# Pooling sums of K and V on GpSimd, written chunk by chunk instead of level by level

## The chip, the cores and the metric

One NeuronCore of a Trainium2 chip runs the whole program in one launch. The metric is the device time of that launch in microseconds; lower is better. PE is TensorE, DVE is VectorE, ACT is ScalarE, POOL is GpSimd and SP is the engine whose queue issues most of the transfers.

## The reference

Three steps, all in float32: an attention whose keys and values are first pooled, a mixture of experts with one expert for each token, and a second feed-forward with a maximum of three products. Only the first step matters for the change. Eight batches, eight heads, 576 rows of 64 values; every eight neighbouring rows of K and of V are averaged into one, which leaves 72 rows for each head.

```python
def _attn_ref(q, k, v):
    B, H, S, D = q.shape            # 8, 8, 576, 64
    pool = 8
    Sp = S // pool                  # 72
    k_p = k.reshape(B, H, Sp, pool, D).mean(axis=3)
    v_p = v.reshape(B, H, Sp, pool, D).mean(axis=3)
    scores = 1.0 / np.sqrt(D) * np.matmul(q, k_p.transpose(0, 1, 3, 2))
    ...
    return np.matmul(attn, v_p)
```

## The kernel before

The program has three stages: attention with the routing of tokens to experts (the first 200 us or so), the expert products, and the second feed-forward. Nothing is scheduled by a tool: each engine runs its instructions in the order in which the code writes them, and waits on semaphores where one needs another's result.

**Attention.** The 4608 tokens are 36 tiles of 128 rows, and the loop at L1477 runs as a pipeline over them. In one turn it writes the scores of one tile (`stage_s`, L415, tile `psc` on PE, then the maximum `mx` and the difference `sh` on DVE), the transposes of an older one (`stage_a`, `paT`), those of a new one (`stage_q`, `pqT`), and the product with V of the oldest (`stage_x`, L482, `pav` on PE, then `rs`, `x`, `dt`, `lg` on DVE). PE may write the next `psc` only when DVE has made `sh` out of the old one, and the next `pav` only when DVE has made `dt`.

**Pooling.** The 576 pooled rows of one batch, 72 for each of 8 heads, lie as four chunks of 128 partitions and a fifth of 64. `load_rows` (L188) brings the raw rows into `kraw` and `vraw`, shape [128, 5, 8, 64]: chunk, the eight rows to be added, 64 values. They are added by halving: the upper four rows onto the lower four (`w` is 4), then two onto two, then one onto one, whose result goes to `kp` (or `vp`). V of all batches and K of batches 2 to 7 are pooled on POOL: `pool_k2` (L263) and `pool_v` (L275). K of batches 0 and 1 is pooled on DVE. `spread_v` (L284) multiplies the pooled V into `vbd`, five POOL instructions for each batch. PE then transposes `kp` into `ptk` (L313, for batches 2 and up) and multiplies with `vbd` in `pav` (L490). The loop calls these steps of a batch at turns that the table at L1464 to L1469 sets: for batch b its pooling stands five turns ahead of the first tile that needs it.

**Routing.** Among the DVE instructions of a turn the loop pushes single steps of the routing (`fill`, L910): constants first, then for each group of tiles (tiles 0 to 8, 9 to 17, 18 to 23) the steps of `rank_steps` (L600). They work on small tiles in SBUF: `lg` scaled and reduced by its maximum, `wt`, `wm`, `oh`, a copy of `oh` into `pre`, four prefix additions `pre<-pre`, later `rk`, `rank`, `ri`, `lb`, `slot`. When the slots of a group are ready, POOL makes one `ohs` for each tile of the group (L656). After the third group an early part of the routing reads the `ohs` of 24 tiles (L751) and starts the loads of the experts' weights.

**The queue of SP.** It is in order too: K and V of a later batch, q, and the stores of finished tiles. A load of `vraw` waits until POOL has read the buffer's old content.

Of the kernel before, what the change touches and what calls it, by code (L numbers as in the profile page):

```python
# [14 lines left out]
A = mybir.AluOpType  # L15
# [6 lines left out]
def attention_moe_moe_kernel(  # L22
# [24 lines left out]
    nc = tc.nc  # L47
    dbg = dbg or {}

    P = 128  # L50
# [65 lines left out]
    if True:  # L116
# [61 lines left out]
        if True:  # L178

            RC = [P, P, P, P, 64]  # L180
# [67 lines left out]
            def prep_steps(b):  # L248
                kt, vt = kv[b]
                kb, vb = kbds[b % 3], vbds[b % 3]  # L250
                kp = qp.tile([P, 5, 2, D], F32, tag="kp", name=f"kp{b}")
                vp = kp[:, :, 1, :] if b > 1 else qp.tile([P, 5, D], F32, tag="vp", name=f"vp{b}")
# [8 lines left out]
                        pool_k(c)  # L261

                def pool_k2():  # L263
                    for c0, c1, n in ((0, 4, P), (4, 5, RC[4])):
                        for w in (4, 2, 1):
                            dst = kt[0:n, c0:c1, 0:w, :] if w > 1 else kp[0:n, c0:c1, 0:1, :]
                            nc.gpsimd.tensor_tensor(
                                dst, kt[0:n, c0:c1, 0:w, :], kt[0:n, c0:c1, w : 2 * w, :], op=A.add
                            )

                def dup_k():
                    for c0, c1, n in ((0, 3, P), (3, 4, KC[3]), (4, 5, KC[4])):
                        nc.scalar.copy(kp[0:n, c0:c1, 1, :], kp[0:n, c0:c1, 0, :])

                def pool_v(c0, c1, n):  # L275
                    for w in (4, 2, 1):
                        for a0 in range(c0, c1, 2) if w == 4 else (c0,):
                            a1 = min(a0 + 2, c1) if w == 4 else c1
                            dst = vt[0:n, a0:a1, 0:w, :] if w > 1 else vp[0:n, a0:a1, :].unsqueeze(2)
                            nc.gpsimd.tensor_tensor(  # L280
                                dst, vt[0:n, a0:a1, 0:w, :], vt[0:n, a0:a1, w : 2 * w, :], op=A.add
                            )

                def spread_v():  # L284
                    for c, (h0, h1) in enumerate(HS):
# [74 lines left out]
                if b == 0:  # L360
                    return [
                        lambda: (pool_all(), dup_k(), trans_k(range(4), 0, 7), trans_k([4], 7, 8)),
                        lambda: (pool_v(0, 4, P), pool_v(4, 5, 64), spread_v()),
                        lambda: (trans_v(0, 4), trans_v(4, 5)),
                        lambda: vdot(),
                    ]
                if b == 1:
                    pk = [lambda c=c: pool_k(c) for c in range(5)]
                    pk += [lambda: (pool_v(0, 4, P), pool_v(4, 5, 64))]
                else:  # L370
                    return [
                        lambda: (pool_k2(), pool_v(0, 4, P), pool_v(4, 5, 64)),
                        spread_v,
                        lambda: trans_kv(range(4), 0),
                        lambda: trans_kv([4], 4 * P),
                        vdot,
                    ]
# [1425 lines left out]
```

## Time and profile before

| | |
|---|---|
| median of 3 runs | 1264.73 us (1262.85 to 1265.89) |
| the profiled execution's own time | 1260.98 us |
| its span | 1259.2 us |
| PE busy | 1215.6 us, 97% of the span |
| DVE busy | 799.2 us, 63% |
| ACT busy | 580.5 us, 46% |
| POOL busy | 318.9 us, 25%, 383 instructions |
| mean granted clock of TensorE | 0.991 |

The profile is one execution of the program. Its page gives the busy time of each engine and its share of the span; other views order the same instructions by time, by group or by stretch, and name for each idle time of an engine the instruction that ended it. The profiled execution was shorter than each of the three timed runs. Shares over the whole span hide the stages: POOL's 25% are over 85% in each stretch of 15 to 17 us between 30 and 92 us, and little after 180 us.

### The profile page before, as it was taken

To read this page: it belongs to the slowest core of one execution; us is meant where nothing else is said; L and a number is where in the kernel's file an instruction comes from. 1 tells how busy PE (TensorE), PEld (TensorE's weight loads), DVE (VectorE), ACT (ScalarE), POOL (GpSimd) and SP (SyncE) were. 2 spreads that over 40 slices of the span, in tenths; PEclk is the share of its full clock that TensorE was granted. 3 is DMA by queue.
4 is the path that set the end of the run, shared out by engine and by line. 5 is a ranking of instruction groups with operands and counts; after the bars stand their busy time and mean duration, and the time that the engine had idled before them with its cause. 6 is when DMAs were issued, how large, how long until landed. Compare 5 with 4: busy or idle time off the path is not lost. (4 is left out here: it accounts for less than half of the span.)

```text
span 1259.2 us, 22318 instructions
## 1 busy us (share of the span) xinstructions
PE 1215.6 (97%) x8251; PEld 1158.0 (92%) x8251; DVE 799.2 (63%) x1575; ACT 580.5 (46%) x1040; POOL 318.9 (25%) x383
## 2 busy tenths in 40 slices
PE   5899899999999999999999999999999999999995
PEld 4788789999999999999999998998998998998994
DVE  6676886797889999898764446345445454454450
ACT  3466465545666676666655333323223323223221
POOL 6985553420212212222000302103103004004001
PEclk9899999999999999999999999999999999999998
DMA  9968246423976445844619666475564673773721
GB/s 252 267 202 236 97 138 217 151 85 32 298 262 226 164 143 203 283 151 137 207 51 350 241 238 242 160 262 205 207 239 182 220 264 153 258 263 124 253 108 52
DMA packets 98038, 246.21 MB, mean 196 GB/s; under 512 B 17100, under 2 KB 58106, under 8 KB 89858
## 3 DMA queue, kind: packets, MB, share of 16 engines
q1 hardware_dynamic: 84770, 189.09, 44.5%
q0 software_dynamic: 13152, 55.62, 13.3%
q8 instruction: 67, 1.10, 0.4%
q14 instruction: 49, 0.40, 0.1%
HBM read 252.23 MB, written 46.98 MB: 238 GB/s over the span
## 5 line engine op out<-in xcount | busy, mean ns | idle before, releaser
L1617 PE MATMUL p<-yhi,wt 128*128 128x384 f32 x1512 | 387.2, 336 | 0.0
L1617 PEld LDWEIGHTS p<-yhi,wt 128*128 128x128 f32 x1512 | 273.4, 188 | 0.6
L1617 PE MATMUL p<-ylo,wt 128*128 128x384 f32 x756 | 254.0, 336 | 0.0
L1625 ACT COPY s<-p 128x384 f32<-128x384 f32 x162 | 77.8, 480 | 221.1 <-PE p L1617 216.8
L1104 PE MATMUL py<-hhi,whi 128*128 128x256 f32 x576 | 164.6, 286 | 0.0
L1104 PE MATMUL py<-hhi,wlo 128*128 128x256 f32 x576 | 163.1, 283 | 1.6 <-DVE wlo L1036 1.6
L1056 PE MATMUL ph<-xhi,whi 128*128 128x256 f32 x576 | 163.8, 284 | 0.7 <-DVE hlo L1072 0.7
L1056 PE MATMUL ph<-xhi,wlo 128*128 128x256 f32 x576 | 163.0, 283 | 0.7 <-DVE wlo L1036 0.7
L1056 PE MATMUL ph<-xlo,whi 128*128 128x256 f32 x576 | 163.0, 283 | 0.0
L1104 PE MATMUL py<-hlo,whi 128*128 128x256 f32 x576 | 162.9, 283 | 0.0
L1617 PEld LDWEIGHTS p<-ylo,wt 128*128 128x128 f32 x756 | 142.1, 188 | 0.5
L1646 DVE TENSOR_TENSOR blk<-p,s 128x384 f32<-128x384 f32 x108 | 59.7, 553 | 113.9 <-PE p L1617 113.9
L1602 POOL DMA_INDIRECT gt<-gbuf,ix x26 | 37.0, 1424 | 312.1 <-DMA ix<-idbuf 305.7
L1104 PEld LDWEIGHTS py<-hhi,wlo 128*128 128x128 f32 x576 | 110.4, 192 | 1.8 <-DVE wlo L1036 1.8
L1056 PEld LDWEIGHTS ph<-xhi,whi 128*128 128x128 f32 x576 | 110.5, 192 | 1.2 <-DVE hlo L1072 0.9
L1056 PEld LDWEIGHTS ph<-xhi,wlo 128*128 128x128 f32 x576 | 110.5, 192 | 0.9 <-DVE wlo L1036 0.9
L1056 PEld LDWEIGHTS ph<-xlo,whi 128*128 128x128 f32 x576 | 110.5, 192 | 0.0
L1104 PEld LDWEIGHTS py<-hlo,whi 128*128 128x128 f32 x576 | 110.5, 192 | 0.0
L1104 PEld LDWEIGHTS py<-hhi,whi 128*128 128x128 f32 x576 | 110.4, 192 | 0.0
L1036 DVE TENSOR_TENSOR wlo<-w2raw,whi 128x1024 fp32r<-128x1024 f32 x84 | 102.2, 1221 | 8.8 <-ACT whi L1034 8.7
L1036 DVE TENSOR_TENSOR wlo<-w1raw,whi 128x1024 fp32r<-128x1024 f32 x67 | 81.8, 1220 | 27.6 <-ACT whi L1034 26.5
L1034 ACT CAST whi<-w2raw 128x1024 fp32r<-128x1024 f32 x88 | 91.8, 1044 | 7.7 <-PE py L1104 4.7
(316 smaller groups left out, 2280.8 us busy)
## 6 DMA issues: line engine op xcount, KB each, us to landing
wt<-wdram SPq DMA_DIRECT2D x51, 1792.0 KB
w1raw<-in_moe_w_dram SPq DMA_DIRECT2D x88, 512.0 KB
w2raw<-in_moe_w_dram SPq DMA_DIRECT2D x88, 512.0 KB
wdram<-wst POOLq DMA_DIRECT2D x9, 1792.0 KB
ybuf<-yo SPq DMA_DIRECT2D x40, 256.0 KB
cvraw<-in_moe_w_dram POOLq DMA_DIRECT2D x36, 256.0 KB
vraw<-in_v_dram SPq DMA_DIRECT2D x8, 1024.0 KB
xbuf<-x SPq DMA_DIRECT2D x16, 512.0 KB
```

The lines of the kernel that those rows point to most:

```text
L1034: nc.scalar.copy(hi, src)
L1036: eng.tensor_tensor(lo, src, hi.bitcast(F32), op=A.subtract)
L1056: nc.tensor.matmul(ps[:, f, :], a_[:, c, fs], b_[:, c, :], start=(n == 0), stop=(n == 3 * DC - 1))
L1104: nc.tensor.matmul(py[:, c // 2, (c % 2) * 256 : (c % 2 + 1) * 256], a_[:, f, c * P : (c + 1) * P], b_[:, f, :], start=(piece == 0 and f = ...
L1602: nc.gpsimd.indirect_dma_start(out=gt[g][:, j : j + 1], out_offset=None, in_=gbuf[:, :], in_offset=bass.IndirectOffsetOnAxis(ap=cols[j], a ...
L1617: nc.tensor.matmul(ps, a_, b_, start=(start and c + n == 0), stop=(c == 1 and n == 2), skip_group_check=True)
L1625: nc.scalar.copy(t, ps)
L1646: tt(src, add[0], add[1], op=A.add)
```

## The change

`pool_k2` and `pool_v` keep the same additions on the same engine. Before, one instruction did a level of the halving for all four full chunks (the first level of V for two chunks at a time). Now each chunk goes through its three levels before the next one begins. The two functions have five lines less, so that later lines have numbers smaller by 5 in the changed kernel.

```diff
--- before.py
+++ after.py
@@ -261,25 +261,20 @@
                         pool_k(c)
 
                 def pool_k2():
-                    for c0, c1, n in ((0, 4, P), (4, 5, RC[4])):
+                    for c, n in enumerate(RC):
                         for w in (4, 2, 1):
-                            dst = kt[0:n, c0:c1, 0:w, :] if w > 1 else kp[0:n, c0:c1, 0:1, :]
-                            nc.gpsimd.tensor_tensor(
-                                dst, kt[0:n, c0:c1, 0:w, :], kt[0:n, c0:c1, w : 2 * w, :], op=A.add
-                            )
+                            dst = kt[0:n, c, 0:w, :] if w > 1 else kp[0:n, c, 0:1, :]
+                            nc.gpsimd.tensor_tensor(dst, kt[0:n, c, 0:w, :], kt[0:n, c, w : 2 * w, :], op=A.add)
 
                 def dup_k():
                     for c0, c1, n in ((0, 3, P), (3, 4, KC[3]), (4, 5, KC[4])):
                         nc.scalar.copy(kp[0:n, c0:c1, 1, :], kp[0:n, c0:c1, 0, :])
 
                 def pool_v(c0, c1, n):
-                    for w in (4, 2, 1):
-                        for a0 in range(c0, c1, 2) if w == 4 else (c0,):
-                            a1 = min(a0 + 2, c1) if w == 4 else c1
-                            dst = vt[0:n, a0:a1, 0:w, :] if w > 1 else vp[0:n, a0:a1, :].unsqueeze(2)
-                            nc.gpsimd.tensor_tensor(
-                                dst, vt[0:n, a0:a1, 0:w, :], vt[0:n, a0:a1, w : 2 * w, :], op=A.add
-                            )
+                    for c in range(c0, c1):
+                        for w in (4, 2, 1):
+                            dst = vt[0:n, c, 0:w, :] if w > 1 else vp[0:n, c : c + 1, :]
+                            nc.gpsimd.tensor_tensor(dst, vt[0:n, c, 0:w, :], vt[0:n, c, w : 2 * w, :], op=A.add)
 
                 def spread_v():
                     for c, (h0, h1) in enumerate(HS):
```

What this does to the order of POOL's instructions is seen at two places. Names in brackets are the semaphores on which an instruction waits; `Pool` is POOL's own. First POOL before, the K rows of batch 2, the first batch whose K it pools:

```order
L267 TENSOR_TENSOR kraw_254<-kraw_254 128x4x256 [waits DMAHW4_49,DMAHW3_49,DMAHW5_49,DMAHW2_49,DVE_49]
L267 TENSOR_TENSOR kraw_254<-kraw_254 128x4x128 [waits Pool_49]
L267 TENSOR_TENSOR kp_484<-kraw_254 128x4x64 [waits PE_49,Pool_49]
L267 TENSOR_TENSOR kraw_254<-kraw_254 64x256 [waits DMAHW3_49]
L267 TENSOR_TENSOR kraw_254<-kraw_254 64x128 [waits Pool_49]
L267 TENSOR_TENSOR kp_484<-kraw_254 64x64 [waits Pool_49]
```

and the same place in the changed kernel, the first three of its five chunks:

```order
L267 TENSOR_TENSOR kraw_262<-kraw_262 128x256 [waits DMAHW4_49,DMAHW3_49,DMAHW5_49,DMAHW2_49,DVE_49]
L267 TENSOR_TENSOR kraw_262<-kraw_262 128x128 [waits Pool_49]
L267 TENSOR_TENSOR kp_500<-kraw_262 128x64 [waits PE_49,Pool_49]
L267 TENSOR_TENSOR kraw_262<-kraw_262 128x256
L267 TENSOR_TENSOR kraw_262<-kraw_262 128x128 [waits Pool_49]
L267 TENSOR_TENSOR kp_500<-kraw_262 128x64 [waits Pool_49]
L267 TENSOR_TENSOR kraw_262<-kraw_262 128x256
L267 TENSOR_TENSOR kraw_262<-kraw_262 128x128 [waits Pool_49]
L267 TENSOR_TENSOR kp_500<-kraw_262 128x64 [waits Pool_49]
```

Three instructions over four chunks have become twelve, of a quarter of the size each. In both, the second and third level wait for the level in front; the first level of a chunk waits for none of POOL's. For K and V of one batch there are 30 instructions where there were 13 (for V alone, in batches 0 and 1, 15 where there were 7); over the program 118 are added.

The second place is where `spread_v` of one batch (here batch 5) stands in front of the K of the next. POOL before:

```order
L288 TENSOR_TENSOR vbd_156<-kp_1137,mslot 128x2x64 [waits PE_49]
L288 TENSOR_TENSOR vbd_156<-kp_1137,mslot 128x3x64 [waits PE_49] x3
L288 TENSOR_TENSOR vbd_156<-kp_1137,mslot 64x64 [waits PE_49,Pool_49]
L267 TENSOR_TENSOR kraw_1156<-kraw_1156 128x4x256 [waits DMAHW6_49]
L267 TENSOR_TENSOR kraw_1156<-kraw_1156 128x4x128 [waits Pool_49]
L267 TENSOR_TENSOR kp_1440<-kraw_1156 128x4x64 [waits PE_49,Pool_49]
```

and now:

```order
L283 TENSOR_TENSOR vbd_156<-kp_1204,mslot 128x2x64 [waits PE_49]
L283 TENSOR_TENSOR vbd_156<-kp_1204,mslot 128x3x64 [waits PE_49] x3
L283 TENSOR_TENSOR vbd_156<-kp_1204,mslot 64x64 [waits PE_49,Pool_49]
L267 TENSOR_TENSOR kraw_1240<-kraw_1240 128x256 [waits DMAHW6_49]
L267 TENSOR_TENSOR kraw_1240<-kraw_1240 128x128 [waits Pool_49]
L267 TENSOR_TENSOR kp_1524<-kraw_1240 128x64 [waits PE_49,Pool_49]
L267 TENSOR_TENSOR kraw_1240<-kraw_1240 128x256
L267 TENSOR_TENSOR kraw_1240<-kraw_1240 128x128 [waits Pool_49]
```

The five instructions of `spread_v` have not moved and have not changed; behind them stands a first level over one chunk instead of four.

## Rows read from the trace of the kernel before

**Rows 1.** Stretches: length, busy PE, PEld, DVE, ACT, POOL (count), PEclk, DMA, GB/s.

```profile
125.00:145.00 20.00, 15.17 (x106) 13.15 (x105) 19.16 (x33) 8.75 (x24) 17.40 (x24) 0.91 0.38 133
...
180.00:1259.20 1079.20, 1062.39 (x7173) 1022.80 (x7172) 668.87 (x1237) 483.35 (x795) 189.80 (x181) 1.00 0.56 194
```

**Rows 2.** Timeline of PE: start, duration, engine, line, work, [idle before <-releaser].

```profile
40.69 0.63 PE L411 MATMUL pqT<-ident,qgrp 128*128 128x128 f32 x4 [2.88 <-DMA qgrp<-in_q_dram]
...
61.52 0.65 PE L313 MATMUL ptk<-ident,kp 128*128 128x128 f32 x4
...
91.57 1.22 PE L436 MATMUL psc<-kbd,qT 128*128 128x144 f32 x8 [2.45 <-DVE pre L547]
...
98.27 2.00 PE L490 MATMUL pav<-vbd,aT 128*128 128x146 f32 x12
...
133.77 3.61 PE L490 MATMUL pav<-vbd,aT 128*128 128x146 f32 x12 [3.16 <-DVE dt L515]
...
142.16 2.07 PE L490 MATMUL pav<-vbd,aT 128*128 128x146 f32 x12 [1.48 <-DVE dt L515]
```

**Rows 3.** Timeline of DVE, same columns, four instructions.

```profile
33.76 4.04 DVE L551 TENSOR_SCALAR im<-iof 128x10 f32<-128x10 f32 x1
...
129.57 3.92 DVE L547 TENSOR_TENSOR oh<-w,wm 128x72 f32<-128x72 f32 x1
...
136.22 0.22 DVE L547 TENSOR_TENSOR pre<-pre 128x72 f32<-128x72 f32 x1
...
137.08 2.62 DVE L547 TENSOR_TENSOR pre<-pre 128x72 f32<-128x72 f32 x1
```

**Rows 4.** Timeline of POOL, same columns; equal neighbours stand in one row.

```profile
33.42 2.04 POOL L288 TENSOR_TENSOR vbd<-vp,mslot 128x128 f32<-128x128 f32 x5
35.42 3.69 POOL L267 TENSOR_TENSOR kraw<-kraw 128x1024 f32<-128x1024 f32 x2
...
47.66 3.70 POOL L267 TENSOR_TENSOR kraw<-kraw 128x1024 f32<-128x1024 f32 x2
...
107.76 7.04 POOL L656 TENSOR_SCALAR ohs<-iof,slot,tokid 128x128 f16<-128x128 f32 x9 [15.49 <-DVE slot L556]
...
131.06 3.67 POOL L267 TENSOR_TENSOR kraw<-kraw 128x1024 f32<-128x1024 f32 x2
...
137.10 3.85 POOL L280 TENSOR_TENSOR vraw<-vraw 128x512 f32<-128x512 f32 x3
...
156.38 0.79 POOL L656 TENSOR_SCALAR ohs<-iof,slot,tokid 128x128 f16<-128x128 f32 x1 [13.04 <-DVE slot L556]
...
174.19 4.99 POOL L656 TENSOR_SCALAR ohs<-iof,slot,tokid 128x128 f16<-128x128 f32 x6 [5.62 <-DVE slot L556]
```

**Rows 5.** DVE by group, 81 to 92 us: xcount | busy us, mean ns | idle.

```profile
L617 DVE COPY pre<-oh 128x72 f32<-128x72 f32 x1 | 2.8, 2753 | 0.0
L547 DVE TENSOR_TENSOR pre<-pre 128x72 f32<-128x72 f32 x4 | 2.1, 522 | 0.0
...
L551 DVE TENSOR_SCALAR lg<-lg,rtau 128x72 f32<-128x72 f32 x1 | 0.7, 665 | 0.0
...
L547 DVE TENSOR_TENSOR lg<-lg,mxl 128x72 f32<-128x72 f32 x1 | 0.2, 224 | 0.0
```

**Rows 6.** DVE by group, 125.5 to 141.1 us, same columns.

```profile
L547 DVE TENSOR_TENSOR pre<-pre 128x72 f32<-128x72 f32 x4 | 4.9, 1222 | 0.0
...
L617 DVE COPY pre<-oh 128x72 f32<-128x72 f32 x1 | 1.2, 1246 | 0.0
```

**Rows 7.** POOL by group and shape, whole span, same columns.

```profile
L280 POOL TENSOR_TENSOR vraw<-vraw 128x512 f32<-128x512 f32 x24 | 30.1, 1267 | 8.8 <-DMA vraw<-in_v_dram 8.2
...
L267 POOL TENSOR_TENSOR kraw<-kraw 128x1024 f32<-128x1024 f32 x6 | 14.1, 2351 | 0.0
...
L267 POOL TENSOR_TENSOR kp<-kraw 128x256 f32<-128x256 f32 x6 | 4.4, 730 | 0.7 <-PE ptk L313 0.4
...
L267 POOL TENSOR_TENSOR kp<-kraw 64x64 f32<-64x64 f32 x6 | 1.9, 316 | 0.5
```

## The prediction

> **What bounds the kernel now.** I read the stretches of the span first. From 180 us to the end PE is busy 1062 of 1079 us at full granted clock [rows 1]: whatever the attention stage gains or loses ahead of that is carried to the end, as long as the expert stage starts by PE's own progress. POOL, which the change touches, is nowhere the bound by its busy time. So the question is where PE stood idle in the attention stage, and that is the timeline of PE [rows 2]: 2.88 us at 40.69 for a load of q, 2.45 us at 91.57 for DVE's `pre`, and 3.16 and 1.48 us at 133.77 and 142.16 for DVE's `dt`. [...] The second group of tiles thus costs 3.16 + 1.48 + 1.61 = 6.25 us on PE, the first 2.45 us.
>
> Next, why DVE was late. One prefix addition takes 0.22 us at 136.22, but 2.62 us at 137.08; `oh` takes 3.92 us at 129.57, and `im`, ten columns, 4.04 us at 33.76 [rows 3]. Now lay POOL's timeline beside it [rows 4]. `im` ends at 37.80. POOL's five `vbd` products began at 33.42 and the first level of `kraw` at 35.42; that level takes 2.35 us [rows 7] and ends at 37.77. `oh` ends at 133.49; the first level that began at 131.06 ends at 133.41. The addition of 137.08 ends at 139.70; two first levels of `vraw` from 137.10 end near 139.60. Each time DVE comes through within 0.1 us of a place where POOL's next instruction waits for the one directly in front. How long is POOL idle there? The pair at 131.06 took 3.67 us, its parts 2.35 and 1.27 us [rows 7], which leaves about 0.06 us; between independent instructions there is nothing. So, by these rows, a DVE instruction that works from SBUF to SBUF is held up while POOL works, and comes through at a dependence on POOL, not merely at an instruction's end: `im` sat through the ends of five products, since no halving stood among them.
>
> [...]
>
> **The change, part by part.**
>
> *POOL's own time.* An addition over 256 elements takes 0.73 us and over 64 elements 0.32 us [rows 7]; between them a line gives 0.45 us for 128. One chunk is 0.73 + 0.45 + 0.32 and two gaps of 0.06, 1.62 us; ten chunks are 16.2 us. Before, K and V of batch 2 took 47.66 - 35.42 = 12.24 us [rows 4]. That is 4.0 us more for each of six batches and about 2.0 for the two with V alone: 28 us on POOL.
>
> *Whether that reaches PE.* Batch 2 is the tightest. V of batch 1 starts on its load in both cases; it ends 2.0 us later, so batch 2 runs from 37.4 to 53.6, and PE wants it at 61.52 [rows 2]: 7.9 us to spare. Batch 3 ends near 69.8, both spreads near 73.9, batch 4 near 90.1, its spread at 92.1, batch 5 near 108.3, half a microsecond behind the slots at 107.76. Batches 6 and 7 follow `ohs` (7.04 us) and the spreads (2.04 us) [rows 4] and end near 133.5 and 152. So the 28 us fit into the two pauses of 15.49 and 13.04 us in which POOL waited for slots, the second group's at 156.38 among them. I cost them at nothing; without this cover they would cost up to all of the 28 us.
>
> *The first 41 us.* V of batch 0 ends 1.9 us later, and SP's next load of `vraw` waits for it; transfers are behind there anyway, and the load of q that ends at 40.69 leaves PE 2.88 us of slack [rows 2]. DVE's constants now meet the spread of batch 0 but `im` loses its 4 us. I take 0; by the clock loss seen behind an idle PE, the bound is 1.6 us either way.
>
> *DVE in the rank steps.* In the first group nine instructions go from SBUF to SBUF [rows 5]: the copy at 2.75 us, four `pre` at 0.52, `lg` 0.67, the shortest 0.22, and `wt` and `oh`, which lie between these ends (0.5 each, my estimate). That is 6.7 us, against 9 x 0.22 = 2.0 free: 4.7 us of waiting. In the second group: `pre` 4 x 1.22, copy 1.25 [rows 6], `oh` 3.92 [rows 3], and three more that I leave at 0.5 each, in all 11.6 us, against 2.0: 9.6 us.
>
> After the change the unbroken stretches are the third level with the next chunk's first, 0.32 + 0.73 = 1.05 us, and the second level alone, 0.45 us, in a period of 1.62 us. A request at a random moment waits on average (1.05² + 0.45²) / (2 x 1.62) = 0.40 us, at most 1.05 us. Nine requests: 3.6 us. So DVE saves 1.1 us in the first group and 6.0 us in the second. On PE I take 1.1 of the 2.45 us, and in the second group 5.2 of the 6.25: with the clock kept up PE asks sooner, and about 1 us of stall should stay, as in the first. Bounds: nothing in the first group and 3 us in the second if the spreads fall badly, all of 2.45 and 6.25 if they fall well.
>
> *New encounters.* The later steps of a group (`rk`, twice `ri`, `lb`, `slot`) ran in POOL's pauses of 15.49 and 13.04 us [rows 4]; now POOL works there. Five requests at 0.40 are 2.0 us on DVE for each group; DVE waits for PE in those turns, and I take 1.6 us as what it has to spare there, an estimate between none and all of the 2.0; so 0.4 us each, 0.8 us in all, with the bounds 0 and 4.
>
> Sum: 1.1 + 5.2 - 0.8 = 5.5 us. The profiled execution took 1260.98 us; with this it would take 1255.5. The median of the runs, 1264.73 us, is 3.75 us above it, so the forecast is **1259.2 us**.
>
> **The rivals.**
>
> *By instruction.* If DVE comes through at each instruction's end, the mean wait becomes (0.73² + 0.45² + 0.32²) / 3.24 = 0.26 us: 9 x 0.26 = 2.3 us, both stalls go nearly whole, and five requests, 1.3 us, fit into what DVE has to spare in the later steps: 2.4 + 6.25 = 8.6 us, **1256.1 us**. For it: only long waits show that an end is not enough, and the short ones would allow it. Against it: `im` and `oh` at 129.57. [...]
>
> *The gain is lost on POOL.* If the quarter-size additions take a tenth more than the line gives, POOL is some 12 us later by batch 7; then `ohs` of the third group, at 174.19 [rows 4], comes after its slots, the early routing and the experts' loads wait, and the gain of DVE ends there: no change, **1264.7 us**. For it: no row shows a 128 x 128 or 128 x 64 addition. Against it: partitions hardly matter in the rows, elements do.
>
> *More meetings than gaps.* Slower: DVE now meets POOL in 28 requests instead of 18. A spread has no gap, so that a request behind it waits up to 0.32 + 2.04 + 0.73 = 3.1 us, and the spread of batch 4 moves to 90 to 92 us, into the first group's last steps; that of batch 6 stays in the second's. If one request in ten meets one, the mean is 0.9 x 0.40 + 0.1 x 3.1 = 0.67 us. Then the first group loses 9 x 0.67 - 4.7 = 1.3, the second gains 9.6 - 6.0 = 3.6, the later steps lose 2 x (3.35 - 1.6) = 3.5, and one idle stretch on PE costs 1.6 at the lower clock: 2.8 us slower, **1267.5 us**. It decides from a mean wait of about 0.6 us on, where these terms cancel.
>
> **How the numbers follow.** What a measurement of this kernel can tell is about 0.2%, 2.5 us. Forecast 0.52, by instruction 0.14, lost on POOL 0.22, more meetings 0.12. Faster is the first two, 0.66; same 0.22; slower 0.12. The range reaches from 1254.6 (the second case, with 1.5 us for the spread of the runs) to 1265.5 (the third with a little of it) and leaves the fourth out. The forecast's own range is 1256 to 1262.
>
> **What the profile after would show.** POOL's additions near 0.73, 0.45 and 0.32 us, in all some 28 us more; no DVE instruction of a few columns over 1.1 us beside the additions, and the 3.16 us stall with its slow `pav` gone; batch 2 pooled some 8 us ahead of its `ptk`. Wrong would be: DVE instructions of 3 us at 90 or 135 us, stalls of PE at `dt` near 107 or 155 us, a POOL that is still pooling when slots are ready for 5 us, or a PE that waits for POOL.

## The result, and the profile after

The changed kernel takes 1250.01 us (median of 4 runs, 1248.74 to 1251.32) against 1264.99 us before on the same chip (4 runs, 1262.85 to 1265.89): ratio 0.9884, 95% interval 0.9867 to 0.9901. That is 15 us, where 5.5 us was forecast, and lies below the range. The profiled execution took 1249.39 us with a span of 1247.7 us. Two later comparisons on other chips gave 0.9898 (0.9877 to 0.9919) and 0.9877 (0.9862 to 0.9892). One execution among the runs below, of levels_gap (1271.06 us), was in a slower state and is left out of its median and its ratio.

First the stretches of the changed kernel, columns as in [rows 1]; the fourth stands against the first of [rows 1].

```profile
0.00:41.00 41.00, 24.70 (x141) 20.71 (x142) 28.61 (x67) 15.49 (x37) 33.52 (x95) 1.00 1.00 281
41.00:80.00 39.00, 38.80 (x297) 34.83 (x296) 25.23 (x65) 26.31 (x68) 35.63 (x75) 1.00 0.85 262
80.00:92.00 12.00, 12.00 (x95) 11.06 (x92) 10.18 (x30) 6.08 (x16) 10.98 (x25) 1.00 0.66 197
125.00:145.00 20.00, 20.00 (x150) 17.78 (x150) 13.83 (x41) 12.04 (x30) 18.20 (x40) 1.00 0.19 73
...
180.00:1247.70 1067.70, 1049.37 (x7059) 1010.71 (x7057) 659.40 (x1206) 475.78 (x779) 186.32 (x179) 1.00 0.56 194
```

From 80 to 92 and from 125 to 145 us PE never stops, at full clock, although POOL is busy nine tenths of both. From the first `px` of the expert stage to the end of the span the two kernels take 1057.2 and 1058.7 us, so the gain lies ahead of it. The timeline of PE, against [rows 2]:

```profile
56.95 0.66 PE L308 MATMUL ptk<-ident,kp 128*128 128x128 f32 x4
...
84.57 1.25 PE L431 MATMUL psc<-kbd,qT 128*128 128x144 f32 x8
...
123.47 2.00 PE L485 MATMUL pav<-vbd,aT 128*128 128x146 f32 x12
...
128.53 2.00 PE L485 MATMUL pav<-vbd,aT 128*128 128x146 f32 x12
...
162.56 2.07 PE L485 MATMUL pav<-vbd,aT 128*128 128x146 f32 x12 [0.93 <-DVE pinc L554]
...
168.02 0.75 PE L746 MATMUL p_early<-ohbe,ohs 128*128 128x10 f16 x24
...
188.97 1.09 PE L1012 MATMUL px<-ident,xrow 128*128 128x128 f32 x8
```

The `psc` that waited 2.45 us for `pre` stands at 84.57 without a wait. The two `pav` that waited 3.16 and 1.48 us for `dt` stand at 123.47 and 128.53, also without one, and both take 2.00 us. New are a wait of 0.93 us at 162.56 and one of 0.36 us behind it; the first goes back to a step of the third group that met the last spread:

```profile
158.62 1.84 DVE L636 CAST ri<-rank 128x6 int32<-128x6 f32 x1
```

```profile
158.54 2.06 POOL L283 TENSOR_TENSOR vbd<-kp,mslot 128x128 f32<-128x128 f32 x5
```

Now DVE by group in the first rank steps (75 to 86.5 us), against [rows 5]:

```profile
L542 DVE TENSOR_TENSOR pre<-pre 128x72 f32<-128x72 f32 x4 | 1.4, 353 | 0.0
...
L542 DVE TENSOR_TENSOR lg<-lg,mxl 128x72 f32<-128x72 f32 x1 | 0.6, 588 | 0.0
L551 DVE SCALAR_TENSOR_TENSOR wt<-lg,w 128x72 f32<-128x72 f32 x1 | 0.5, 497 | 0.0
L612 DVE COPY pre<-oh 128x72 f32<-128x72 f32 x1 | 0.4, 435 | 0.0
...
L542 DVE TENSOR_TENSOR oh<-w,wm 128x72 f32<-128x72 f32 x1 | 0.3, 304 | 0.0
L546 DVE TENSOR_SCALAR lg<-lg,rtau 128x72 f32<-128x72 f32 x1 | 0.3, 251 | 0.0
```

The nine instructions take 3.5 us in all, where the forecast had 2.0 free and 3.6 of waiting; the second group, 117 to 129.5 us, takes 3.2 us, with the same 353 ns for `pre<-pre`. And POOL by form and by time:

```profile
L277 POOL TENSOR_TENSOR vraw<-vraw 128x256 f32<-128x256 f32 x32 | 23.3, 727 | 3.5 <-DMA vraw<-in_v_dram 3.5
...
L277 POOL TENSOR_TENSOR vraw<-vraw 128x128 f32<-128x128 f32 x32 | 14.7, 458 | 2.5
...
L267 POOL TENSOR_TENSOR kp<-kraw 128x64 f32<-128x64 f32 x24 | 7.7, 321 | 1.9
```

```profile
34.44 1.25 POOL L267 TENSOR_TENSOR kraw<-kraw 128x256 f32<-128x256 f32 x2
...
50.57 1.25 POOL L267 TENSOR_TENSOR kraw<-kraw 128x256 f32<-128x256 f32 x2
...
105.09 7.00 POOL L651 TENSOR_SCALAR ohs<-iof,slot,tokid 128x128 f16<-128x128 f32 x9
...
161.17 4.99 POOL L651 TENSOR_SCALAR ohs<-iof,slot,tokid 128x128 f16<-128x128 f32 x6 [0.57 <-DVE slot L551]
```

0.73, 0.46 and 0.32 us, and 50.57 - 34.44 = 16.13 us for a batch, as forecast (16.2). The pauses of 15.49 and 13.04 us are gone; ahead of the last `ohs` POOL waits 0.57 us. Those `ohs` end at 166.16 us, and PE comes to them at 168.02. These 1.86 us are no different from before (179.18 and 181.04 us); what the change has used up is POOL's own wait for the last slots, 5.62 us before [rows 4]. POOL could be some 0.57 + 1.86 = 2.4 us later before PE waits for it, and less in other executions: in c_after, below, it does not wait for those slots at all, and 0.3 us lie between the last `ohs` and PE.

### The profile page after: what moved, and what is told of

It reads as the page before. It is cut to its first block, busy times and chain, and to the rows that moved or that the text cites. A ratio compares the mean times of both kernels' runs of the same rounds, so it can differ in the third digit from the quotient of the medians.

```text
span 1247.7 us, 22435 instructions
## 1 busy us (share of the span) xinstructions
PE 1211.0 (97%) x8251; PEld 1154.3 (93%) x8251; DVE 789.4 (63%) x1575; ACT 579.9 (46%) x1040; POOL 337.8 (27%) x501
## 5 line engine op out<-in xcount | busy, mean ns | idle before, releaser
L1031 DVE TENSOR_TENSOR wlo<-w1raw,whi 128x1024 fp32r<-128x1024 f32 x67 | 81.9, 1222 | 28.2 <-ACT whi L1029 27.1
```

What stands on the lines that cost most here:

```text
L1031: eng.tensor_tensor(lo, src, hi.bitcast(F32), op=A.subtract)
```

## The experiments

Every run is read at two marks on PE: the first `ptk` of batch 2, and the first `px` of the expert stage. Between them PE's work is the same in all kernels (130 us at full clock), so that what differs is PE's idle time and the clock. Behind `px` all profiles of whole kernels take 1057 to 1061 us to the end of the span. "Time" is the median (c_before and c_after ran once); ratios are to runs of the kernel before on the same chip.

| run | time us | ratio, 95% | ptk at | ptk to px us | PE idle in it | clock in it |
|---|---|---|---|---|---|---|
| before | 1264.99 | | 61.52 | 140.47 | 8.46 | 0.99 |
| c_before | 1263.81 | | 59.53 | 143.68 | 7.03 | 0.95 |
| changed | 1250.01 | 0.9884 (0.9867 to 0.9901) | 56.95 | 132.02 | 2.06 | 1.00 |
| c_after | 1248.08 | | 55.91 | 132.17 | 1.84 | 1.00 |
| c_after_b | 1251.01 | 0.9898 (0.9877 to 0.9919) | 59.70 | 132.75 | 2.40 | 1.00 |
| c_after_c | 1247.35 | 0.9877 (0.9862 to 0.9892) | 58.28 | 132.00 | 2.04 | 1.00 |
| first_two | 1265.83 | 1.0009 (0.9986 to 1.0032) | 57.49 | 145.38 | 8.93 | 0.95 |
| from_two | 1248.39 | 0.9880 (0.9855 to 0.9906) | 56.83 | 132.01 | 2.05 | 1.00 |
| levels | 1280.24 | 1.0136 (1.0102 to 1.0169) | 57.58 | 160.23 | 23.06 | 0.91 |
| zigzag | 1260.86 | 0.9982 (0.9964 to 1.0000) | 58.59 | 147.13 | 8.82 | 0.93 |
| levels_gap | 1260.84 | 0.9962 (0.9932 to 0.9992) | 70.20 | 131.47 | 1.39 | 1.00 |
| levels_gap2 | 1249.31 | 0.9894 (0.9869 to 0.9920) | 53.97 | 134.81 | 4.25 | 1.00 |
| pairs | 1259.50 | 0.9975 (0.9960 to 0.9990) | 57.08 | 140.58 | 8.05 | 0.98 |
| pairs_gap | 1248.77 | 0.9872 (0.9845 to 0.9899) | 55.39 | 133.46 | 2.68 | 1.00 |
| pairs_gap_b | 1247.96 | 0.9879 (0.9857 to 0.9902) | 54.82 | 132.44 | 1.88 | 1.00 |
| after_gap | 1259.85 | 0.9961 (0.9943 to 0.9980) | 54.09 | 146.60 | 8.32 | 0.93 |
| after_gap01 | 1250.32 | 0.9903 (0.9889 to 0.9917) | 54.62 | 138.12 | 5.23 | 0.98 |

**Both kernels again** (c_before and c_after, no edit).

> The kernel before, unchanged, for a second profile of its first 62 us. If the idle time of 2.88 us for q at 40.69 us and the two stretches at half clock (24.8 to 28.2 and 41.9 to 48.7 us) belong to the program, they stand here again, within half a microsecond of their places, and batch 2's transposes ptk near 61.5 us; the two waits for DVE (2.45 us at 91.57, 3.16 us at 133.77) too. If they are chance of the first transfers, ptk of batch 2 comes between 57 and 61 us, and part of what the change seems to win ahead of 62 us isn't its own.

> The changed kernel once more, for a second profile. If the earlier ptk of batch 2 (56.95 us) belongs to the change, it stands within half a microsecond of 57 again; if it hangs on the first transfers, it moves by up to 2 us with the start of POOL's additions to V of batch 0 (14.29 us in the first profile). Either way PE should be idle for 2.0 to 2.2 us in all between that ptk and the first px, with no half clock there, since each gap on POOL lets DVE in.

In c_before both waits for DVE are back (2.45 us at 89.57, 3.19 us at 133.46). The 2.88 us for q are not; PE waits for ACT and DVE instead. Nor do the two early stretches at half clock (0.50 in the first profile, from 24.8 to 28.2 and from 41.9 to 48.7 us) stand in their places: `pd` takes 1.28 us at 24.85, as it does outside them in the first profile, and the `pav` at 42.40 takes 2.00 us, where one took 3.03 at 41.15. A `psc` of 2.26 instead of 1.25 us stands at 28.64, and `ptk` comes at 59.53: what lies ahead of `ptk` differs between executions. So does the clock behind the second stall:

```profile
125.00:145.00 20.00, 16.62 (x95) 14.83 (x92) 18.20 (x29) 8.85 (x24) 17.10 (x24) 0.74 0.34 118
```

0.74 in the stretch that [rows 1] show at 0.91. The stall is the same; what the lower clock costs in this stretch is, by my estimate from these means, (1 - 0.74) x 20 = 5.2 us here and 1.8 us there. With the change the marks lie 132.0 to 132.8 us apart in all four profiles, at full clock and with 1.84 to 2.40 us of idle time (2.0 to 2.2 expected). `ptk` moves between 55.91 and 59.70 us, and not with the start of POOL's additions alone: in c_after they begin 0.93 us later than in the first profile (15.22 after 14.29), and `ptk` comes 1.04 us earlier.

**Level by level** (levels): the change's additions, in an order in which none waits for the one directly in front. For V likewise.

```diff
-                    for c, n in enumerate(RC):
-                        for w in (4, 2, 1):
+                    for w in (4, 2, 1):
+                        for c, n in enumerate(RC):
```

> The additions of the change, the same shapes and the same count, written level by level over all five chunks, so that no addition waits for the one directly in front. Theory of the gaps (DVE comes through where POOL's next instruction waits for the one in front): POOL now has no gap in the 15 us of a batch, DVE instructions of 5 us and more appear in the rank steps, PE stalls grow over those of before, and the time is 1270 us or more. Theory of the short instructions (any end of an instruction lets DVE in, and the change only made the instructions short): no DVE instruction in the rank steps over 1 us, time 1249 to 1251 us, as with the change.

30 us slower than the changed kernel, with the same instructions. DVE and POOL of this run:

```profile
79.87 0.21 DVE L554 TENSOR_REDUCE mxl<-lg 128x9 f32<-128x72 f32 x1
...
82.00 7.40 DVE L542 TENSOR_TENSOR oh<-w,wm 128x72 f32<-128x72 f32 x1
...
89.46 6.39 DVE L612 COPY pre<-oh 128x72 f32<-128x72 f32 x1
```

```profile
82.20 2.04 POOL L283 TENSOR_TENSOR vbd<-kp,mslot 128x128 f32<-128x128 f32 x5
84.21 5.50 POOL L267 TENSOR_TENSOR kraw<-kraw 128x256 f32<-128x256 f32 x10
89.68 1.42 POOL L267 TENSOR_TENSOR kp<-kraw 128x64 f32<-128x64 f32 x5
91.06 5.10 POOL L277 TENSOR_TENSOR vraw<-vraw 128x256 f32<-128x256 f32 x9
```

`oh` sat through the ends of fourteen instructions, none longer than 0.72 us, and came through at 89.29, at an end without a gap where the next instruction works on 64 partitions. That POOL's additions became short is thus not enough to explain the gain.

**Two changes of direction** (zigzag): as levels, but the second level runs through the chunks backwards.

```diff
-                        for c, n in enumerate(RC):
+                        for c in range(5) if w != 2 else range(4, -1, -1):
+                            n = RC[c]
```

> The same 30 additions for each batch as in the run level by level, but the second level goes through the chunks backwards, so that at each change of level POOL's next instruction works on the chunk just finished: two gaps for K and two for V of a batch where that run had none. Theory of the gaps: DVE gets in at each of the four, the longest unbroken stretches are 3 to 6 us, much as before the change, and the time falls from 1280 us to 1262 to 1270 us. Theory that an instruction's end lets DVE in by chance, gap or not: nothing changes, 1277 to 1283 us.

1260.86 us: two gaps for K and two for V give back 19 us and bring it to where the kernel before stood. The longest DVE instructions of its rank steps take 4.87 and 4.96 us (at 80.66 and 135.46), where levels has 7.40.

**Added work on POOL** (levels_gap, levels_gap2): levels, with copies of one element that leave gaps.

```diff
+                            if b > 3 and (w, c) in GAPS:
+                                nc.gpsimd.tensor_copy(tiny, dst[0:1, 0, 0:1])
```

> The run level by level (1280 us) with work added to POOL and none taken away: in batches 4 to 7 a copy of one element stands behind eight of the fifteen additions to K and eight of those to V, and behind the second and fourth product of every spread. Each copy reads what the instruction directly in front has written, so that it waits and leaves a gap; the longest stretch without one is 1.4 us. Theory of the gaps: DVE comes through at each, the stalls of PE go, and the time falls by some 25 us to 1249 to 1256 us (up to 5 us are left for stretches that join badly). Theory of the order or the size: more instructions on POOL in the same order can only hold DVE up more, 1280 us or above.

Between the marks it is 131.47 us with 1.39 us idle, where levels took 160.23; the 25 us are there. The total (1250.10 to 1266.92 us) misses. In the profile the loss lies ahead of `ptk`, where batches 2 and 3 had no copies. There stood

```profile
34.78 12.22 DVE L554 TENSOR_SCALAR im<-iof 128x10 f32<-128x10 f32 x1
```

and PE stalled 8.83 us at 48.32 for the `dt` queued behind it. With copies in batches 2, 4, 5 and 6:

> Level by level again, with the copies of one element where the DVE instructions that waited longest fall: in batches 2, 4, 5 and 6 (batch 2 had none in the run before, and there one DVE instruction of ten columns took 12.22 us and PE stalled 8.83 us), five copies in K and five in V instead of eight, and one in each spread, so that POOL is hardly later than with the change. Theory of the gaps: no DVE instruction beside POOL over 2.3 us, PE idle under 3.5 us and no half clock between batch 2's ptk and the first px, 1249 to 1254 us where the same additions without the copies took 1280 us. If gaps don't decide, 1262 us or more.

1249.31 us. Its longest waits on PE are 1.55 and 1.31 us for `dt`, behind an `oh` of 1.23 us in each group. Two of the bounds were missed: idle time is 4.25 us instead of 3.5, and `rk` took 3.24 us at 138.86 instead of at most 2.3, beside additions of batch 7, which had no copies; PE did not wait there. Levels and levels_gap2 do the same additions in the same order; copies that compute nothing save 31 us.

**Either part alone** (first_two, from_two): the chunked V loop only for batches 0 and 1, or chunked K and V only from batch 2 on.

```diff
+                    if b < 2:
+                        for c in range(c0, c1):
+                            for w in (4, 2, 1):
...
+                    else:
+                        for w in (4, 2, 1):
```

> Chunk by chunk only for V of batches 0 and 1, all ahead of 42 us; the rest level by level as before. If the change itself wins the 4.6 us by which the transposes ptk of batch 2 came earlier (56.95 after 61.52 us), ptk stands at 57 us here too, the two stalls for DVE at 91 and 134 us stay at 2.4 and 3.2 us, and the time is 1260 to 1261 us. If that gain is chance of the first transfers, or comes from batches 2 and up, the time is 1264 to 1266 us.

> The other part alone: chunk by chunk for K and V of batches 2 to 7, V of batches 0 and 1 as before. If the two parts add up, the stalls for DVE near 91 and 134 us are gone, ptk of batch 2 stays near 61.5 us, and the time is 1254 to 1256 us. If the first 62 us gain nothing of their own, it is 1249 to 1251 us, as with the whole change.

from_two has the whole gain. In first_two `ptk` came at 57.49 us, 4 us ahead of [rows 2], and nothing is left of it: its first group of tiles waits

```profile
82.44 1.95 PE L428 MATMUL psc<-kbd,qT 128*64 128x144 f32 x16 [2.94 <-DVE mxl L565]
...
90.89 1.22 PE L442 MATMUL psc<-kbd,qT 128*128 128x144 f32 x8 [1.60 <-DVE pre L553]
```

4.54 us for DVE instead of 2.45. In this profile, with POOL's gaps still rare behind 42 us, a PE that was early waited longer.

**Two chunks at a time** (pairs, and pairs_gap with copies in the spreads).

```diff
+                    for c0, c1, n in ((0, 2, P), (2, 4, P), (4, 5, RC[4])):
...
+                        if c in (0, 1, 2, 3):
+                            nc.gpsimd.tensor_copy(tiny, vb[0:1, SL[c], 0:1])
```

> Three levels over two chunks at a time, for K and V: 18 additions for a batch instead of 30. Longest unbroken stretch 0.45 + 1.27 = 1.72 us where the change has 1.05, mean wait of a DVE request at a random moment 0.66 us where it has 0.40. If DVE's requests come at random moments and PE waits for their sum, the two rank groups lose some 2.3 us each on DVE, PE stalls by 1 to 2 us in each, and the time is 1252 to 1255 us. If requests fall in step with the gaps and DVE has time to spare, it is 1248.5 to 1251 us, as with single chunks.

1259.50 us: both theories missed it, and most of the gain is gone. Two DVE instructions of this run:

```profile
79.15 2.58 DVE L547 TENSOR_TENSOR lg<-lg,mxl 128x72 f32<-128x72 f32 x1
...
126.82 3.52 DVE L617 COPY pre<-oh 128x72 f32<-128x72 f32 x1
```

```profile
127.03 2.04 POOL L288 TENSOR_TENSOR vbd<-kp,mslot 128x128 f32<-128x128 f32 x5
129.03 2.06 POOL L267 TENSOR_TENSOR kraw<-kraw 128x512 f32<-128x512 f32 x2
```

The copy asks at 126.82, sits through the spread and the first level behind it, and comes through near 130.3. With less work on POOL the spreads come earlier (127.03 us, 130.23 in the changed kernel) and fall into the rank steps.

> The run with two chunks at a time (1259.5 us), its additions unchanged, with the same copy of one element behind each of the first four products of a spread. In that run the two long DVE instructions (lg of 2.58 us at 79.15 and the copy into pre of 3.53 us at 126.82) each sat through a whole spread and the first level behind it. If the spread is what its missing gain went to, the longest DVE instruction of the rank steps is 1.7 us, PE's stalls near 84 and 134 us fall under 1 us, and the time is 1249 to 1252 us. If the pair's longer stretches cost it by themselves, it stays at 1257 to 1260 us.

1248.77 us: 32 copies of one element are worth 11 us here, 13 by the ratios, as the two ran on different chips. The longest DVE instructions are 1.68 us, as expected.

**Gaps in the changed kernel's own spreads** (after_gap).

> The changed kernel with the same copies in its spreads. With single chunks the rank steps meet no spread in the traces (they end at 84.5 and 129.5 us, the spreads run from 86.9 and 130.2 us), so by the theory of the gaps only constants in the first 41 us gain: 1248 to 1251 us, no difference that can be measured. If meeting spreads still costs the changed kernel something in some executions, 1246 to 1248 us.

Some 10 us slower than the changed kernel, against both expectations. DVE is not the main reason: PE waits 2.7 us for it behind `ptk`, 1.3 in the changed kernel. PE and POOL of this run:

```profile
168.44 0.67 PE L749 MATMUL p_early<-ohbe,ohs 128*128 128x10 f16 x18
170.86 0.19 PE L749 MATMUL p_early<-ohbe,ohs 128*128 128x10 f16 x1 [1.75 <-POOL ohs L654]
...
174.73 0.19 PE L749 MATMUL p_early<-ohbe,ohs 128*128 128x10 f16 x1 [0.58 <-POOL ohs L654]
```

```profile
156.32 0.80 POOL L654 TENSOR_SCALAR ohs<-iof,slot,tokid 128x128 f16<-128x128 f32 x1
...
170.01 4.67 POOL L654 TENSOR_SCALAR ohs<-iof,slot,tokid 128x128 f16<-128x128 f32 x6
```

The third group's `ohs` begin at 170.01 us instead of 161.17, and PE waits for them one by one, 4.7 us in all; the granted clock is 0.80 from 140 to 190 us, 1.00 in the changed kernel. This is the forecast's rival of a POOL that is late: the changed kernel stands 0.3 to 2.4 us away from it.

**The first stage alone** (after_gap01: the copies only where `b < 2`).

> The changed kernel with copies of one element in the spreads of batches 0 and 1 alone (eight copies in all, ahead of 36 us), so that POOL is only 2 us later. In the profiles so far batch 2's ptk came 44 to 45 us after POOL's first addition to V of batch 0 before the change, 41 to 43 us after it with the change, and 39 to 40 us with gaps in the spreads. If the constants that meet those spreads cost the first stage, this one shows 39 to 40 us too, and is 1.5 to 3 us faster than the changed kernel beside it, 1247 to 1249.5 us; if that order is chance of the first transfers, both take the same time.

`ptk` comes at 54.62 us, 39.9 us behind POOL's first addition, as expected; the total does not follow (1250.32 against 1247.35 us for the changed kernel beside it). In its profile, what is won ahead of 55 us goes at the last spread:

```profile
161.06 1.80 DVE L545 TENSOR_TENSOR texc<-pinc,pf 128x8 f32<-128x8 f32 x1
```

`texc` asks just after the spread of batch 7 has begun (160.95), and the `psc` at 166.01 waits 2.84 us for DVE, whose steps behind `texc` are late by it. It is the meeting that `ri` has in the changed kernel, at a dearer place.

**The best of them beside the changed kernel** (pairs_gap_b, c_after_b, c_after_c).

> Two chunks at a time with copies in the spreads, again, beside the changed kernel on the same chip. 18 additions instead of 30 for a batch leave POOL earlier at the third group's slots. If the changed kernel loses nothing to POOL, both take the same time, 1248 to 1250.5 us; if its small slack (its last ohs ends at 166.16 us, PE's first p_early comes at 168.02 us) is used up in some executions, this one is 1 to 3 us faster.

> The changed kernel, for the comparison on the same chip: 1248.5 to 1251 us, PE idle about 2 us between batch 2's ptk and the first px, no half clock there.

> The changed kernel for the comparison: 1248.5 to 1251.5 us, and 41 to 43 us between the first addition to V of batch 0 and batch 2's ptk.

On one chip pairs_gap is 3 us faster (1247.04 to 1249.70 against 1250.65 to 1252.12), the upper end of what was expected, but between the marks the two profiles differ by 0.3 us; the rest lies ahead of `ptk`, where V of batch 0 was pooled from 15.40 and from 16.80 us. The changed kernel took 1247.35 us in the next comparison, on another chip, a little below what was expected. No version beats it for certain.

**Less to add** (last_only: for batches 2 to 7 only the last level of the halving).

> A bound for what is left: for batches 2 to 7 the first two levels of the halving are left out (two rows of eight are added instead of all), which takes POOL's additions for a batch from 16 to about 3.3 us. If the waits of DVE for POOL that are left with the change still cost PE something, the time is 1246 us or less; if the change has already hidden them all, it is 1248 to 1250.5 us.

The total (1411.88 us) can't be compared: what lies behind the first `px` takes 1409.1 - 189.47 = 1219.6 us, most likely because other pooled values route the tokens otherwise. The stretch between the marks can be read:

```profile
58.29:189.47 131.18, 129.86 (x1002) 116.60 (x1000) 94.19 (x292) 85.04 (x215) 47.60 (x92) 1.00 0.57 185
```

1.32 us idle against 1.84 to 2.40: with the spreads still in place, what the additions still cost the changed kernel there is some 0.5 to 1.1 us.

## Why the prediction was wrong

The mechanism was right in the main: DVE is held while POOL works (`oh` took 7.40 us in levels, 0.30 in the changed kernel), POOL's gaps let it through (207 times, and none was sat through), and PE stops waiting (7.09 us of stalls went). POOL's 28 us (16.13 us for a batch, 16.2 forecast) and their cover were right too. The size was wrong, by three terms that all erred to the same side.

- **"On PE I take 1.1 of the 2.45 us, and in the second group 5.2 of the 6.25."** All of both went, and the "about 1 us of stall" that should stay in each did not. The step that failed is the mean wait of 0.40 us, and under it the premise that DVE comes through "not merely at an instruction's end". Nine requests took 3.5 us in the first group, 2.0 of them free: 0.17 us of waiting each; over both groups in all four profiles of the changed kernel it is 0.14 to 0.27 us, 0.20 on average. The traces show which half of the formula was wrong. Had each of these 72 requests, at the moment at which it was made, waited for the next gap, the mean would have been 0.39 us, just what the formula gives for random moments. But in each group two or three of the nine, 20 of the 72 in all, came through at an end without a gap, each time between a third level and the first level of the next chunk, which the formula counts as one unbroken stretch. The bound "all of 2.45 and 6.25 if they fall well" was the outcome, but not because the requests fell well.
- **The clock, 1.61 us.** It is 3.61 less 2.00 us, of the two `pav` at 133.77 and 98.27 in [rows 2]; the granted clock was 0.53 in the first and 1.00 in the second. I took it from the one execution shown. That one had the smallest loss: between the marks PE is busy 132.01 us in it, 136.65 in c_before and 136.45 in first_two, for 130 us of work. In the stretch with the stall of 3.2 us the lower clock cost, by the estimate above, some 1.8 us in one profile and 5.2 in the next, and with the change neither comes (1.00 from 125 to 145 us). The profiled execution was 3.75 us shorter than the median, and I carried that difference over to the forecast unchanged. Part of it is likely the very loss that went away: c_before took 2.83 us more than the profiled execution, and 3.21 more between the marks.
- **"The first 41 us. I take 0."** `ptk` comes at 60.5 us on average in two profiles before and at 57.7 in four of the change, 2.8 us earlier, with 2.0 and 3.8 us between profiles of one kernel; part of it may be chance. The 2.88 us at 40.69 were also misread: they are no slack of the load of q, but PE waiting for it [rows 2], and in c_before they are gone without any change. Nor does the clock ahead of `ptk` follow the change: the eight products of a `psc` that take 1.25 us at full clock take 2.26 to 2.29 us in all six profiles (at 25.10 and 28.64 us before, at 24.94, 29.19, 25.20 and 30.98 with the change; the 1.00 that the changed kernel shows for 0 to 41 us misses this). `ptk` is early in first_two (57.49) and in from_two (56.83) alike, so the runs pin it on neither part, and first_two shows that without the rest it is worth nothing.
- **"New encounters", 0.8 us lost**, was nearly right: the new waits are 0.93 and 0.36 us, and one of 0.59 us that the kernel before had at 166.86 is gone, which leaves 0.70 us. The larger one came at a spread, not at the additions.

So the account of the 15 us is this. Between the marks 140.47 - 132.02 = 8.45 us went: 7.09 of stalls (2.45, 3.16 and 1.48) and 2.05 of clock, less the 0.70. Ahead of `ptk` it is 4.57 us, and behind `px` 1.5 us were lost; that makes 11.5 between the two profiled executions. The rest is that the one before lay 4.0 us under its median of four, and the one after 0.6 us.

Of the rivals, "by instruction" gave 1256.1 us and a mean wait of 0.26 us, nearer than the forecast, and the 20 of 72 are its mechanism. As a rule it is refuted by levels (1280 us): there instructions ended every 0.3 to 0.7 us, and `oh` waited 7.40 us, through the ends of fourteen of them. VectorE was thus held beyond the end of the instruction that held it. What decides whether it comes through at an end without a gap stays open. "More meetings than gaps" did not come with the change, but its mechanism is real: in pairs, where two long DVE instructions met a spread, most of the gain was gone (1259.50 us), and it came back with gaps in the spreads (1248.77 us). "Lost on POOL" is what after_gap shows.

## What to carry to other kernels

When a short VectorE instruction takes microseconds, look at whether GpSimd is streaming beside it, and count GpSimd's pauses, not its busy time: here an order in which each instruction needs the one in front let VectorE through (pauses of 0.08 us; 1250.01 us where levels took 1280.24), and a copy of one element that depends on the last result did the same (0.17 to 0.25 us each; 1248.77 us in pairs_gap where pairs took 1259.50). Spend that only where VectorE's late steps stop PE, and see what GpSimd owes next: here 0.3 to 2.4 us of slack stood between a gain of 15 us and one of 4. A stall on PE was dearer here than its idle time: in the stretch with the 3.2 us the clock was 0.91 in one profile and 0.74 in the other (by my estimate 1.8 and 5.2 us), so one profile was not enough to price it.

## What was not expected of the hardware

Laid against each other over all profiles of whole kernels, the DVE instructions on the rank tiles and constants that took 0.37 us or more (20 to 180 us) came through at a gap of POOL 207 times, and never did one sit through a gap. At ends without a gap they came through 34 of 82 times where the next POOL instruction works on 64 partitions after one on 128, and 34 of 272 times elsewhere. A wider choice of DVE instructions gives 224 times at a gap, again with none that sat through one, and 39 of 82 and 54 of 337 at the two kinds of end. I expected none at either kind of end; why it came through more often at the step to 64 partitions was not tried. One thing sets a gap apart in the records: POOL's next addition begins 0.08 us behind the end of the one that it needs, but some 0.04 us ahead of the end of one that it does not need (0.077 to 0.079 us at 185 of 186 gaps and 0.033 to 0.047 us at 74 other ends in the first profiles of both kernels). That this overlap is what keeps DVE out is not shown.

DVE's reductions in the rank steps were not held: `mxl` took 0.21 us at 79.87 in levels, between instructions that took 0.8 to 7 us, and 0.21 to 0.22 us over 72 columns in the ten profiles read for it. Nor were the two long instructions that read PSUM (`sh` 0.74 to 0.76 us and `x` 0.68 to 0.69 us from 20 to 180 us in the first profiles of both kernels).
